# The head of a linear-attention and two-feed-forward kernel in another emission order

## The chip, the cores and the metric

The kernel runs on 1 core of one Trainium2 chip. The metric is device time in microseconds (us) of one execution; three runs of the kernel before took 870.92, 872.31 and 872.92 us.

## The reference

Inputs are r, k, v of shape (4, 8, 768, 48) (batch B, heads H, steps S, head width D), w and u of shape (8, 48), and two pairs of weight matrices. All is float32.

```
state = 0                                    # (B, H, 48, 48)
for t in range(768):
    cur = (u * k_t) outer v_t
    y_t = r_t @ (state + cur)
    state = w * state + k_t outer v_t
x = y as (3072 tokens, 384 features)
h = x @ w_in   (384 x 2048);  g = max(h, 0) + alpha * min(h, 0);  x = g @ w_out  (2048 x 384)
h = x @ w_in2  (384 x 2048);  g = h * tanh(log(1 + exp(h)));      out = g @ w_out2
```

## The kernel before, in words

**Attention in units.** The 768 steps are cut into 6 chunks of 128. Units 0 to 3 are the first chunk of the four batches; each has its own load of r and k (turned, `rk`), and of v and k (`nat`). From unit 4 on a unit is half a chunk (64 steps) of two batches. A unit is: scores r·k on TensorE (`scores`), a mask and the u-term put over them (`preset`, `masked`), the product with v (`attend0`, `batch`), and the running state (`states_first`, `t_decay`, `t_update`). The decay is carried by tables of powers of w that `tables` computes on VectorE; `load_RKs` (four DMAs from SBUF to SBUF) copies them from the layout of pairs of heads into the layout of seats that units from 4 on use.

**The feed-forward layers in slots.** A layer has 6 blocks of 512 tokens times 16 slices of the hidden width: 96 slots. A slot is `mA_h` (9 matmuls into a PSUM bank `h`), `mA_g` (ScalarE, then VectorE, from `h` to `g`; after it the bank is free), `mA_hi` and `mA_lo` (g split in two rounded parts, ScalarE and VectorE) and `mA_out` (9 matmuls). Block 0 needs units 0 to 3, so slot 0 starts when all four are through. There are two `h` banks, and a unit from 4 on takes one of them too, from its `batch` until `x_parts` has read it out.

**Weights.** Each of the 16 weight slices of layer 1 comes in raw (768 KB, `more_raw`, `load_raw`), is scaled on ScalarE (`w_scale`, two instructions), joined on VectorE (`w_join`) and split in two parts (`w_hi`, `w_lo`). From slot 15 on, the weights of layer 2 come the same way, one slice per four slots: `load_raw 1 f`, `w_scale (1,f)`, `w_join (1,f)`, `w2_store f` back to DRAM.

**Order.** Every step is a closure with a place in slots: `at(place, work, ...)` (L823). A dictionary `PLACES` (L60 on) replaces places by name, and `run_plan` (L833) sorts by place and calls the steps. The order of calls is the order in which instructions stand in each engine's queue, and each queue is worked off in order: a step that waits holds back all that stands behind it on its engine. All loads and stores of this part stand in one queue, that of SyncE (SP). Semaphores are set by the framework. Between two steps on different engines the order of calls matters only where one needs the other's data or buffer.

**Steps that the prediction follows.** `keep_warm` (L592) is a pair of filler matmuls; 8 calls stand ahead of everything, and 10 single calls are in `PLACES` as `keep_warm 3` with 0 to 9 marks `#`. `mA_end 0` (L646) copies the three sums of block 0 out of PSUM (ScalarE, VectorE, ScalarE) and stores them with one DMA. `t_decay 8` runs on ScalarE (four instructions, by the entry `?decay 8`), `preset 9 0` and `preset 9 1` on ScalarE (four each), `prep_c2 9` on VectorE (one sum).

```
    def run_plan():
        for place, _, work, args in sorted(plan, key=lambda p: p[:2]):
            work(*args)
```

Of the kernel before, what the change touches and what calls it, by code (L numbers as in the profile page):

```python
# [54 lines left out]
def more_state(u):  # L55
# [5 lines left out]
    "tables": -133.8283, "dma_start": -128.3432, "load_unit 1": -128.1527, "load_unit 0": -125.2362,  # L61
    "load_unit 2": -124.1803, "load_unit 3": -121.8174, "pad_v 1": -119.5623, "m_first 0": -118.998,
    "c_first 0": -117.2355, "dma_start#": -115.5868, "more_raw 3": -115.5854, "memset": -115.5721,
    "load_k 1": -115.4582, "tensor_scalar": -115.426, "dma_start##": -115.3727, "pad_v 0": -115.2759,
    "load_k 2": -115.0763, "load_k 0": -114.1881, "prep_rk 0": -113.5294, "keep_warm 3####": -111.4759,
    "<lambda> 0": -111.3741, "scale_Kn": -109.6007, "<lambda> 2": -108.8137, "w_scale (0,0)": -108.7521,
# [8 lines left out]
    "preset_first 2": -97.6565, "w_join (0,0)": -97.4588, "c_first 3": -97.3694, "w_hi (0,0) False": -96.6418,  # L75
# [7 lines left out]
    "half_tables": -88.7279, "preset 4 0": -86.4962, "x_first_lo 1": -85.1599, "w_hi (0,1) False": -84.3399,  # L83
# [3 lines left out]
    "mA_h 1": -10.0052, "w_hi (0,2) False": -9.0297, "scores 4": -7.6474, "w_join (0,3)": -7.6021,  # L87
# [4 lines left out]
    "w_lo (0,3)": 1.8993, "batch 4": 1.9228, "tables_seat": 1.9613, "mA_out 0": 2.0723, "w_join (0,4)": 2.1732,  # L92
    "mA_hi 1": 2.2917, "w_scale (0,5)": 2.2957, "mA_lo 1": 2.3517, "prep_kn 5": 2.3844, "prep_pair 6 0": 2.5634,
    "w_hi (0,4) False": 2.6901, "mA_h 2": 2.7398, "w_lo (0,4)": 2.8443, "mA_g 2": 2.9067, "w_join (0,5)": 2.9707,
    "more_raw 8": 2.9931, "more_raw 9": 3.0346, "t_decay 4": 3.0928, "mA_hi 2": 3.1982, "w_hi (0,5) True": 3.2114,
# [6 lines left out]
    "batch 5": 4.9611, "w_hi (0,6) False": 5.1766, "w_scale (0,8)": 5.2656, "more_raw 11": 5.4186, "mA_hi 5": 5.4234,  # L102
# [5 lines left out]
    "w_hi (0,9) True": 7.2287, "more_raw 13": 7.3665, "w_lo (0,8)": 7.3825, "mA_h 7": 7.4985, "mA_g 7": 7.5512,  # L108
    "masked 6 0": 7.5749, "w_lo (0,9)": 7.6299, "prep_c2 7": 7.6723, "mA_out 6": 7.7202, "mA_hi 7": 7.7615,
    "mA_lo 7": 7.9068, "w_join (0,10)": 7.9852, "preset 7 0": 7.9988, "mA_h 8": 8.1558, "prep_kn 6": 8.2758,  # L110
    "mA_g 8": 8.2832, "more_raw 14": 8.5104, "w_hi (0,10) False": 8.5586, "batch 6": 8.605, "x_parts 6": 8.6069,
# [6 lines left out]
    "w_hi (0,12) False": 11.0336, "prep_kn 7": 11.1115, "mA_hi 11": 11.1167, "w_lo (0,12)": 11.263,  # L118
# [3 lines left out]
    "batch 7": 12.4901, "w_hi (0,13) True": 12.5785, "x_parts 7": 12.6986, "load_unit 9": 12.7519,  # L122
# [935 lines left out]
```

## Time and profile before

| what | us |
|---|---|
| median of 3 runs | 872.31 (870.92 to 872.92) |
| profiled execution, its span from first to last instruction | 870.2 |
| TensorE (PE) busy in the span | 861.3 (99%) |
| VectorE (DVE) busy | 631.9 (73%) |
| ScalarE (ACT) busy | 616.2 (71%) |
| GpSimd (POOL) busy | 106.9 (12%) |

The profile shows one execution, of which it gives the span; what lies around the span is in the times of the runs. Busy PE includes the filler matmuls and the time in which a matmul is in flight. The chain of waits that ended last is 93% PE; its other parts (4% DMA) lie in the first 45 us. Each row of a timeline is: start us, length us, engine, source line, operation, out<-in, shapes, count, and in brackets the idle time of the engine before it and what ended it. Instructions of one engine overlap a little, so the distance from start to start is shorter than the length. "SPq" is SyncE's queue that issues DMAs.

### The profile page before, as it was taken

How to read it: one execution, taken by the hardware profiler on the slowest of the kernel's cores; microseconds unless marked ns; L12 is line 12 of the kernel's file. 1: busy time of each engine (PE TensorE's matmuls, PEld its weight loads, DVE VectorE, ACT ScalarE, POOL GpSimd, SP SyncE). 2: the span in 40 equal slices, each digit the busy share in tenths (PEclk: the TensorE clock that was granted, in tenths of full speed). 3: DMA queues.
4: the chain of work that ended last, by engine and by line, in shares of the span. 5: the costliest groups of instructions: out<-in, count | busy, mean ns of one | idle time of the engine just before them, and what ended most of it. 6: DMA issues, size and time to landing. Idle time of an engine off the chain costs nothing.

```text
span 870.2 us, 16712 instructions
## 1 busy us (share of the span) xinstructions
PE 861.3 (99%) x6380; PEld 712.1 (82%) x6380; DVE 631.9 (73%) x1012; ACT 616.2 (71%) x1174; POOL 106.9 (12%) x121
## 2 busy tenths in 40 slices
PE   9899999999999999999999999999999999999998
PEld 6678878888888888888888888888888888888897
DVE  6888855657656565554665887887887887887875
ACT  3797755454445545444555998998998998998886
POOL 4744222111122111100002000000000000000000
PEclk9999999999999999999999999999999999999999
DMA  8967464254444526211621200110110110100101
GB/s 317 277 210 216 111 195 140 82 170 157 136 131 141 143 86 209 77 56 64 205 87 35 110 1 1 26 48 1 26 48 1 24 51 0 27 12 1 26 12 37
DMA packets 65840, 80.41 MB, mean 92 GB/s; under 512 B 39712, under 2 KB 52960, under 8 KB 65760
## 3 DMA queue, kind: packets, MB, share of 16 engines
q1 hardware_dynamic: 65200, 79.24, 29.9%
q8 instruction: 50, 0.82, 0.4%
q14 instruction: 30, 0.25, 0.1%
q10 hardware_dynamic: 560, 0.10, 0.1%
HBM read 61.16 MB, written 15.73 MB: 88 GB/s over the span
## 4 chain that ended last, share of the span: by engine, by line
PE 93%; DMA 4%; ACT 1%; SPq 1%; DVE 0%; issue 0%; POOL 0%; ACTq 0%; DVEq 0%; POOLq 0%
PE h L238 44%; PE acc L643 22%; PE sc L764 8%; PE acc L764 8%; PE yt L764 4%; PE acc L762 3%; DMA rk<-in_rkT 1%; DMA nat<-in_nat 1%; PE sc L457 1%; PE sc L762 1%; DMA wrawr<-in_w 1%; PE h L488 1%; PE yt L509 1%; DMA w15u<-in_nat 1%; PE sc L502 1%; PE yt L488 1%
## 5 line engine op out<-in xcount | busy, mean ns | idle before, releaser
L238 PE MATMUL h<-x,w 128*128 128x512 f32 x1728 | 415.6, 390 | 2.3 <-DVE w L163 1.3
L238 PEld LDWEIGHTS h<-x,w 128*128 128x128 f32 x1728 | 323.8, 188 | 71.4 <-DVE w L163 2.1
L643 PE MATMUL acc<-ghi,w 128*128 128x512 f32 x516 | 175.2, 394 | 0.0
L611 ACT ACTIVATE m<-h 128x512 f32<-128x512 f32 x96 | 57.2, 596 | 87.5 <-PE h L238 87.4
L643 PEld LDWEIGHTS acc<-ghi,w 128*128 128x128 f32 x516 | 96.8, 188 | 21.3
L613 DVE SCALAR_TENSOR_TENSOR g<-m,oma,h 128x512 f32<-128x512 f32 x96 | 71.6, 746 | 57.7 <-ACT m L611 56.6
L160 ACT ACTIVATE ghi<-g 128x512 fp32r<-128x512 f32 x86 | 54.1, 629 | 76.1 <-PE acc L643 46.1
L643 PE MATMUL acc<-glo,w 128*128 128x512 f32 x258 | 100.5, 389 | 0.0
L163 DVE TENSOR_TENSOR glo<-g,ghi 128x512 fp32r<-128x512 f32 x86 | 60.2, 700 | 51.8 <-ACT ghi L160 51.7
L701 DVE SCALAR_TENSOR_TENSOR a<-ghi,h 128x512 f32<-128x512 f32 x96 | 66.1, 688 | 37.8 <-ACT ghi L698 31.3
L701 DVE SCALAR_TENSOR_TENSOR g<-s,c 128x512 f32<-128x512 f32 x95 | 66.7, 702 | 22.7 <-ACT s L698 20.6
L709 ACT ACTIVATE m<-h 128x512 f32<-128x512 f32 x96 | 56.4, 588 | 35.0 <-PE h L238 35.0
L163 DVE TENSOR_TENSOR gloB<-g,ghiB 128x512 fp32r<-128x512 f32 x105 | 72.0, 686 | 6.8 <-ACT ghiB L160 6.8
L698 ACT ACTIVATE ghi<-m,biases 128x512 f32<-128x512 f32 x96 | 69.6, 725 | 3.2
L160 ACT ACTIVATE ghiB<-g 128x512 fp32r<-128x512 f32 x105 | 64.8, 617 | 8.8 <-PE acc L643 6.9
L698 ACT ACTIVATE glo<-ghi,biases 128x512 f32<-128x512 f32 x96 | 68.1, 710 | 0.1
L698 ACT ACTIVATE s<-glo,biases 128x512 f32<-128x512 f32 x96 | 68.1, 709 | 0.0
L698 ACT ACTIVATE s<-s,biases 128x512 f32<-128x512 f32 x96 | 68.0, 708 | 0.0
L764 PE MATMUL sc<-ghiB,w 128*128 128x512 f32 x192 | 66.9, 389 | 0.0
L701 DVE SCALAR_TENSOR_TENSOR b<-ghi,a 128x512 f32<-128x512 f32 x96 | 65.7, 685 | 0.1
L701 DVE SCALAR_TENSOR_TENSOR c<-glo,b 128x512 f32<-128x512 f32 x95 | 65.7, 692 | 0.0
L764 PE MATMUL acc<-ghiB,w 128*128 128x512 f32 x192 | 61.7, 389 | 0.0
(184 smaller groups left out, 1161.3 us busy)
## 6 DMA issues: line engine op xcount, KB each, us to landing
wrawr<-in_w SPq DMA_DIRECT2D x28, 768.0 KB, 4.9
nat<-in_nat SPq DMA_DIRECT2D x40, 288.0 KB, 4.2
w2d<-wj SPq DMA_DIRECT2D x16, 384.0 KB, 2.5
wraw<-w2d SPq DMA_DIRECT2D x16, 384.0 KB, 3.0
rk<-in_rkT SPq DMA_DIRECT2D x40, 128.0 KB, 2.9
x2d<-xo SPq DMA_DIRECT2D x6, 768.0 KB, 3.4
x<-x2d SPq DMA_DIRECT2D x6, 768.0 KB, 4.4
rk<-in_rkT SPq DMA_DIRECT2D x40, 96.0 KB, 2.7
```

Of the source, the lines that this page charges most:

```text
L160: act.activation(out=hi, in_=src, func=AF.Copy)
L163: eng.tensor_tensor(out=lo, in0=src, in1=hi.bitcast(F32), op=ALU.subtract)
L238: pe.matmul(h, w_in(layer, f, a, c), x[:, b, c, :], start=(k == 0), stop=(k == 3 * KC - 1))
L488: pe.matmul(y[i][64 * q:64 * q + 64, p * HC:(p + 1) * HC], T[ROWS[h], 2 * bp + i, k, :], pair[i][ROWS[h], 0, k, t], start=(r == 0 and not ...
L611: act.activation(out=m, in_=hA[s], func=AF.Relu, scale=-1.0)
L613: dve.scalar_tensor_tensor(out=g, in0=m, scalar=oma[:, f:f + 1], in1=hA.pop(s), op0=ALU.mult, op1=ALU.add)
L643: pe.matmul(acc[0][c], w_out(0, f, a)[:, c * 128:(c + 1) * 128], g[b], start=(f == 0 and k == 0), stop=(f == NF - 1 and k == 2))
L698: act.activation(out=out, in_=in_, func=AF.Square, scale=scale, bias=fin[bias])
L701: dve.scalar_tensor_tensor(out=out, in0=in0, scalar=scalar, in1=in1, op0=op0, op1=ALU.mult)
L709: act.activation(out=bnew("t", n), in_=v["h", n], func=AF.Tanh, scale=0.5)
L762: pe.matmul(acc[1][t][:, :DM], g[a][:, t * C:(t + 1) * C], w_out(1, f, b), **se)
L764: pe.matmul(acc[1][t], w_out(1, f, a)[:, t * 128:(t + 1) * 128], g[b], **se)
```

## The change

Only `PLACES` changes: all entries for steps up to slot 18 get new places, between 1.699 and 17.999, 0.05 apart. The set of steps is the same, and so is everything from `mA_h 18` on. The order of the new dictionary is the order of the calls. Its core (lines left out are of the same kind):

```diff
-    "tables": -133.8283, "dma_start": -128.3432, "load_unit 1": -128.1527, "load_unit 0": -125.2362,
...
-    "m_first 3": -99.4133, "load_RKs": -98.9853, "scores 1": -98.8978, "preset_first 1": -98.86, "masked 1 0": -98.78,
...
-    "masked 8 0": 14.6804, "t_update 7": 14.7869, "mA_lo 14": 14.7896, "load_raw 1 0": 14.8571, "masked 8 1": 14.8651,
...
-    "mA_hi 16": 16.883, "prep_kn 9": 17.1837, "t_decay 8": 17.205, "preset 9 0": 17.3813, "preset 9 1": 17.3858,
-    "x_parts 8": 17.9208, "load_unit 11": 18.7912,
+    "?lo 2": 1, "?decay 4": 1, "?preset 3": 1, "?lo 4": 1, "load_unit 0": 1.699, "pad_v 0": 1.749, "tables": 1.799,
+    "scale_Kn": 1.849, "m_first 0": 1.899, "c_first 0": 1.949, "load_unit 1": 1.999, "<lambda> 1": 2.049,
...
+    "masked 2 1": 4.399, "masked 2 0": 4.449, "load_k 2": 4.499, "c_first 3": 4.549, "load_RKs": 4.599,
+    "keep_warm 3##": 4.649, "keep_warm 3########": 4.699, "keep_warm 3#": 4.749, "scores 3": 4.799, "w_lo (0,0)": 4.849,
...
+    "load_unit 4": 5.899, "prep_pair 4 0": 5.949, "dma_start#": 5.999, "tensor_scalar": 6.049, "prep_kn 1": 6.099,
+    "states_first 0": 6.149, "half_tables": 6.199, "keep_warm 3###": 6.249, "keep_warm 3#########": 6.299,
+    "keep_warm 3": 6.349, "load_unit 5": 6.399, "x_first_lo 3": 6.449, "w_hi (0,2) False": 6.499, "more_raw 7": 6.549,
+    "x_first_lo 1": 6.599, "mA_h 0": 6.649, "mA_h 1": 6.699, "tables_seat": 6.749, "prep_pair 4 1": 6.799,
...
+    "w_join (0,4)": 7.699, "more_raw 8": 7.749, "more_raw 9": 7.799, "more_raw 10": 7.849, "keep_warm 3#####": 7.899,
+    "keep_warm 3#######": 7.949, "mA_hi 1": 7.999, "prep_c 5": 8.049, "mA_lo 1": 8.099, "mA_g 2": 8.149,
...
+    "prep_kn 8": 16.899, "mA_hi 15": 16.949, "mA_lo 15": 16.999, "mA_g 16": 17.049, "masked 8 1": 17.099,
+    "mA_out 15": 17.149, "mA_end 0": 17.199, "load_raw 1 0": 17.249, "mA_hi 16": 17.299, "mA_lo 16": 17.349,
+    "batch 8": 17.399, "x_parts 8": 17.449, "w_scale (1,0)": 17.499, "w_join (1,0)": 17.549, "prep_c2 9": 17.599,
+    "preset 9 0": 17.649, "preset 9 1": 17.699, "prep_kn 9": 17.749, "t_decay 8": 17.799, "t_update 8": 17.849,
+    "mA_g 17": 17.899, "mA_hi 17": 17.949, "w2_store 0": 17.999, "load_unit 11": 18.7912,
```

Steps that had no entry before keep their place by rule there: `mA_h 17` 17, `mA_g 17` 17.55, `mA_out 15` 17.68, `mA_end 0` 17.681, `w_scale (1,0)` and `w_join (1,0)` 17.69. With that, the queues near slot 18 read:

```
PE  before:  ... mA_out 14, batch 8, mA_h 17, mA_out 15, mA_h 18, mA_out 16, mA_h 19
PE  after:   ... mA_out 14, mA_h 17, mA_out 15, batch 8, mA_h 18, mA_out 16, mA_h 19
ACT before:  t_decay 8, preset 9 0, preset 9 1, mA_g 17, mA_end 0, w_scale (1,0), mA_hi 17, x_parts 8, mA_g 18
ACT after:   mA_end 0, mA_hi 16, x_parts 8, w_scale (1,0), preset 9 0, preset 9 1, t_decay 8, mA_g 17, mA_hi 17, mA_g 18
DVE after:   mA_end 0, mA_lo 16, x_parts 8, w_join (1,0), prep_c2 9, t_update 8, mA_g 17, mA_lo 17
SP  before:  load_unit 9, load_unit 10, load_raw 1 0, mA_end 0, w2_store 0, x_parts 8, load_unit 11
SP  after:   load_unit 9, load_unit 10, mA_end 0, load_raw 1 0, x_parts 8, w2_store 0, load_unit 11
```

And near slot 0, from `attend0 3` on:

```
PE  before:  attend0 3, states_first 0, keep_warm, mA_h 0, mA_h 1, scores 4, states_first 2, batch 4, mA_out 0, mA_h 2, mA_out 1
PE  after:   attend0 3, states_first 0, 3 keep_warm, mA_h 0, mA_h 1, scores 4, mA_h 2, 2 keep_warm, mA_out 0, batch 4, mA_out 1
```

In the queue before, all 10 `keep_warm` calls stand ahead of `mA_h 0`; in the queue after, 8 of them. `states_first 2` stands ahead of `mA_h 0` after.

## Rows read from the trace of the kernel before

**Rows 1.** Busy time by stretch: length, busy us (count) by engine, granted clock, DMA.

```profile
9.06:32.59 23.53, 23.36 (x334) 17.68 (x332) 18.66 (x23) 12.48 (x34) 13.56 (x13) 1.00 0.97 309
43.67:119.33 75.66, 74.86 (x808) 61.12 (x802) 61.46 (x101) 58.25 (x129) 29.74 (x26) 1.00 0.59 176
```

**Rows 2.** Timeline of PE ahead of slot 0: a filler call, scores, states.

```profile
19.72 0.89 PE L596 MATMUL acc<-ghi 128*128 128x384 f32 x2
20.55 1.10 PE L457 MATMUL sc<-w12u 48*64 48x64 f32 x32
...
31.31 0.53 PE L538 MATMUL acc<-w9u 128*48 128x48 f32 x16
...
32.13 0.91 PE L596 MATMUL acc<-ghi 128*128 128x384 f32 x2
```

**Rows 3.** Timeline of PE from slot 0 to slot 4: where it waited.

```profile
36.83 1.89 PE L238 MATMUL h<-x,w 128*128 128x512 f32 x7 [1.27 <-DVE w L163]
39.66 0.69 PE L457 MATMUL sc<-rk 48*64 48x64 f32 x32 [0.94 <-DVE rk L381]
40.29 0.56 PE L538 MATMUL acc<-w13u 128*48 128x48 f32 x16
...
41.63 0.27 PE L488 MATMUL h<-rk,T 48*64 48x64 f32 x1 [0.42 <-DVE g L613]
...
43.67 0.50 PE L643 MATMUL acc<-ghi,w 128*128 128x512 f32 x1
...
52.94 0.93 PE L238 MATMUL h<-x,w 128*128 128x512 f32 x3 [0.80 <-DVE x L163]
```

**Rows 4.** Timeline of DVE: the first product with the seats' tables.

```profile
34.11 1.80 DVE L381 TENSOR_TENSOR rk<-rk,RKs 112x1024 f32<-112x1024 f32 x1 [1.50 <-DMA RKs<-RK]
```

**Rows 5.** Timeline of PE around batch 8 and slots 15 to 18.

```profile
113.03 0.27 PE L488 MATMUL h<-rk,T 48*64 48x64 f32 x1
...
114.94 2.35 PE L238 MATMUL h<-x,w 128*128 128x512 f32 x9
117.13 0.39 PE L643 MATMUL acc<-ghi,w 128*128 128x512 f32 x1
...
119.17 2.20 PE L238 MATMUL h<-x,w 128*128 128x512 f32 x9
```

**Rows 6.** Timeline of SyncE's queue at the end of block 0.

```profile
109.88 0.58 SPq L180 DMA_DIRECT2D wrawr<-in_w  x1
119.99 0.34 SPq L653 DMA_DIRECT2D x2d<-xo  x1
122.53 0.32 SPq L214 DMA_DIRECT2D w2d<-wj  x1
```

**Rows 7.** Raw loads issued at 89.90 and at 109.88: us to landing.

```profile
DMA to landing us min/median/max: 4.3/4.3/4.3
DMA to landing us min/median/max: 6.3/6.3/6.3
```

**Rows 8.** Timeline of ACT around the end of block 0.

```profile
114.51 1.17 ACT L518 ACTIVATE T<-T,w 112x96 f32<-112x96 f32 x4 [0.48 <-PE h L488]
115.59 2.02 ACT L428 ACTIVATE Ah<-cst,cc 128x64 f32<-128x64 f32 x8
...
119.86 0.89 ACT L186 ACTIVATE wrawr<-wrawr 128x768 f32<-128x768 f32 x1
120.65 0.87 ACT L187 ACTIVATE wrawr<-wrawr 128x768 uint32<-128x768 uint32 x1
...
121.93 0.21 ACT L160 ACTIVATE y<-yt 112x64 fp32r<-112x64 f32 x1
...
122.56 0.62 ACT L611 ACTIVATE m<-h 128x512 f32<-128x512 f32 x1
```

**Rows 9.** Timeline of DVE: a sum for the u-term, then the end of block 0.

```profile
30.36 0.55 DVE L416 TENSOR_REDUCE cc<-nat 128x8 f32<-128x384 f32 x1
...
121.55 0.96 DVE L192 SCALAR_TENSOR_TENSOR wj<-wrawr 128x768 uint32<-128x768 uint32 x1 [2.07 <-ACT wrawr L187]
...
123.14 0.35 DVE L163 TENSOR_TENSOR x<-h,x 112x192 fp32r<-112x192 f32 x1
...
125.14 0.74 DVE L613 SCALAR_TENSOR_TENSOR g<-m,oma,h 128x512 f32<-128x512 f32 x1
```

**Rows 10.** Busy time after the last matmul: PE busy 0.00, granted clock 0.92.

```profile
868.00:870.30 2.30, 0.00 (x0) 0.00 (x0) 0.00 (x0) 0.00 (x0) 0.00 (x0) 0.92 0.32 106
```

More of the change, by code (lines that the diff above doesn't have):

```diff
@@ L60 @@
 PLACES = {
-    "tables": -133.8283, "dma_start": -128.3432, "load_unit 1": -128.1527, "load_unit 0": -125.2362,
[L62 to L65, printed above, removed]
@@ L66 @@
-    "<lambda> 0": -111.3741, "scale_Kn": -109.6007, "<lambda> 2": -108.8137, "w_scale (0,0)": -108.7521,
[8 rows of a table removed]
-    "preset_first 2": -97.6565, "w_join (0,0)": -97.4588, "c_first 3": -97.3694, "w_hi (0,0) False": -96.6418,
[7 rows of a table removed]
-    "half_tables": -88.7279, "preset 4 0": -86.4962, "x_first_lo 1": -85.1599, "w_hi (0,1) False": -84.3399,
[3 rows of a table removed]
-    "mA_h 1": -10.0052, "w_hi (0,2) False": -9.0297, "scores 4": -7.6474, "w_join (0,3)": -7.6021,
[4 rows of a table removed]
-    "w_lo (0,3)": 1.8993, "batch 4": 1.9228, "tables_seat": 1.9613, "mA_out 0": 2.0723, "w_join (0,4)": 2.1732,
@@ L93 @@
-    "mA_hi 1": 2.2917, "w_scale (0,5)": 2.2957, "mA_lo 1": 2.3517, "prep_kn 5": 2.3844, "prep_pair 6 0": 2.5634,
-    "w_hi (0,4) False": 2.6901, "mA_h 2": 2.7398, "w_lo (0,4)": 2.8443, "mA_g 2": 2.9067, "w_join (0,5)": 2.9707,
-    "more_raw 8": 2.9931, "more_raw 9": 3.0346, "t_decay 4": 3.0928, "mA_hi 2": 3.1982, "w_hi (0,5) True": 3.2114,
[6 rows of a table removed]
-    "batch 5": 4.9611, "w_hi (0,6) False": 5.1766, "w_scale (0,8)": 5.2656, "more_raw 11": 5.4186, "mA_hi 5": 5.4234,
[5 rows of a table removed]
-    "w_hi (0,9) True": 7.2287, "more_raw 13": 7.3665, "w_lo (0,8)": 7.3825, "mA_h 7": 7.4985, "mA_g 7": 7.5512,
@@ L109 @@
-    "masked 6 0": 7.5749, "w_lo (0,9)": 7.6299, "prep_c2 7": 7.6723, "mA_out 6": 7.7202, "mA_hi 7": 7.7615,
-    "mA_lo 7": 7.9068, "w_join (0,10)": 7.9852, "preset 7 0": 7.9988, "mA_h 8": 8.1558, "prep_kn 6": 8.2758,
-    "mA_g 8": 8.2832, "more_raw 14": 8.5104, "w_hi (0,10) False": 8.5586, "batch 6": 8.605, "x_parts 6": 8.6069,
[6 rows of a table removed]
-    "w_hi (0,12) False": 11.0336, "prep_kn 7": 11.1115, "mA_hi 11": 11.1167, "w_lo (0,12)": 11.263,
[3 rows of a table removed]
-    "batch 7": 12.4901, "w_hi (0,13) True": 12.5785, "x_parts 7": 12.6986, "load_unit 9": 12.7519,
@@ L123 @@
-    "mA_hi 12": 12.8252, "w_hi (0,14) False": 12.9398, "mA_out 11": 12.9799, "w_lo (0,14)": 12.9935,
-    "w_lo (0,13)": 13.2622, "w_scale (0,15)": 13.3173, "prep_c 9": 13.3735, "mA_h 13": 13.5197, "mA_h 14": 13.5472,
-    "w_join (0,15)": 13.6724, "w_hi (0,15) True": 13.8183, "load_unit 10": 13.8272, "mA_lo 12": 13.8955,
[7 rows of a table removed]
+    "?pair 8 0": 1, "?hi 7": 1, "?hi 3": 1, "?decay 8": 1, "?hi 15": 1, "?decay 9": 1, "?warm 5": 1, "?lo 13": 1,
+    "?lo 2": 1, "?decay 4": 1, "?preset 3": 1, "?lo 4": 1, "load_unit 0": 1.699, "pad_v 0": 1.749, "tables": 1.799,
@@ new lines @@
+    "scale_Kn": 1.849, "m_first 0": 1.899, "c_first 0": 1.949, "load_unit 1": 1.999, "<lambda> 1": 2.049,
+    "preset_first 0": 2.099, "load_k 0": 2.149, "m_first 1": 2.199, "c_first 1": 2.249, "preset_first 1": 2.299,
+    "prep_rk 1": 2.349, "dma_start": 2.399, "table_Kn 0": 2.449, "prep_rk 0": 2.499, "scores 0": 2.549,
+    "load_unit 2": 2.599, "m_first 2": 2.649, "c_first 2": 2.699, "masked 0 0": 2.749, "masked 0 1": 2.799,
+    "load_unit 3": 2.849, "m_first 3": 2.899, "keep_warm 3####": 2.949, "more_raw 3": 2.999, "w_scale (0,0)": 3.049,
@@ new lines @@
+    "keep_warm 3######": 3.099, "pad_v 2": 3.149, "dma_start##": 3.199, "pad_v 3": 3.249, "prep_rk 2": 3.299,
[3 rows of a table added]
+    "x_first 0": 4.149, "w_scale (0,1)": 4.199, "w_join (0,1)": 4.249, "w_hi (0,0) False": 4.299, "scores 2": 4.349,
[6 rows of a table added]
+    "load_unit 4": 5.899, "prep_pair 4 0": 5.949, "dma_start#": 5.999, "tensor_scalar": 6.049, "prep_kn 1": 6.099,
+    "states_first 0": 6.149, "half_tables": 6.199, "keep_warm 3###": 6.249, "keep_warm 3#########": 6.299,
+    "keep_warm 3": 6.349, "load_unit 5": 6.399, "x_first_lo 3": 6.449, "w_hi (0,2) False": 6.499, "more_raw 7": 6.549,
[6 rows of a table added]
@@ new lines @@
+    "mA_out 0": 8.199, "w_hi (0,3) True": 8.249, "w_lo (0,3)": 8.299, "w_scale (0,5)": 8.349, "w_join (0,5)": 8.399,
+    "load_unit 7": 8.449, "w_hi (0,4) False": 8.499, "prep_kn 4": 8.549, "batch 4": 8.599, "x_parts 4": 8.649,
[4 rows of a table added]
+    "mA_h 4": 9.699, "mA_g 4": 9.749, "mA_out 2": 9.799, "mA_out 3": 9.849, "w_hi (0,5) True": 9.899,
[3 rows of a table added]
+    "w_join (0,8)": 10.699, "w_hi (0,7) True": 10.749, "w_lo (0,7)": 10.799, "mA_hi 5": 10.849, "mA_lo 5": 10.899,
+    "prep_kn 5": 10.949, "batch 5": 10.999, "mA_g 6": 11.049, "t_decay 5": 11.099, "t_update 5": 11.149,
@@ new lines @@
+    "w_scale (0,9)": 11.199, "x_parts 5": 11.249, "mA_hi 6": 11.299, "mA_lo 6": 11.349, "w_hi (0,8) False": 11.399,
[4 rows of a table added]
+    "w_hi (0,9) True": 12.449, "w_hi (0,10) False": 12.499, "w_lo (0,10)": 12.549, "preset 6 1": 12.599,
+    "masked 6 1": 12.649, "prep_c2 7": 12.699, "mA_g 8": 12.749, "mA_hi 8": 12.799, "prep_kn 6": 12.849,
+    "mA_lo 8": 12.899, "batch 6": 12.949, "w_lo (0,9)": 12.999, "t_decay 6": 13.049, "w_scale (0,12)": 13.099,
+    "w_join (0,12)": 13.149, "w_scale (0,11)": 13.199, "w_join (0,11)": 13.249, "w_hi (0,11) True": 13.299,
[3 rows of a table added]
@@ L133 @@
+    "mA_out 10": 14.149, "w_hi (0,12) False": 14.199, "w_lo (0,12)": 14.249, "mA_h 12": 14.299, "w_join (0,13)": 14.349,
[4 rows of a table added]
+    "mA_out 12": 15.399, "prep_c 8": 15.449, "w_hi (0,14) False": 15.499, "w_lo (0,14)": 15.549, "mA_h 14": 15.599,
+    "mA_g 13": 15.649, "w_scale (0,15)": 15.699, "w_join (0,15)": 15.749, "mA_hi 13": 15.799, "mA_lo 13": 15.849,
+    "mA_out 13": 15.899, "w_hi (0,15) True": 15.949, "w_lo (0,15)": 15.999, "mA_h 15": 16.049, "mA_h 16": 16.099,
[8 rows of a table added]
 }
```

76 rows, old and new, of the table PLACES are left out of this document.

## The prediction

> **What bounds the kernel now.** The page comes first: PE is busy 861.3 of 870.2 us, the next engine 631.9, and the chain of waits is PE for 93%. Nothing that only shortens work on another engine can show. Then the busy time by stretch: from 9.06 to 32.59 us PE is busy 23.36 of 23.53, fillers included, and from 43.67 to 119.33, 74.86 of 75.66 [rows 1]. In such a stretch the end of the kernel is the sum of PE's work, so an order can change the time in two ways only: it takes away a place where PE waits, or it makes one. The third view, PE's timeline, tells where it waits before: between the two stretches, 1.27 us ahead of the second half of `mA_h 1`, 0.94 ahead of `scores 4`, 0.42 ahead of `batch 4`, and 0.80 at 52.94 [rows 3]. These are 3.4 us in all, and the change moves steps around each of them. The last views are the queues at slots 15 to 19, where PE does not wait before; there I look for waits that the new order makes.
>
> **The head: what goes.** Up to `mA_h 0` PE has the same work in both orders but for two things: `states_first 2` comes ahead of it (+0.82, from 31.31 to 32.13) and two filler calls go behind it (2 × 0.83, from 19.72 to 20.55) [rows 2]. If PE waits nowhere, `mA_h 0` starts at 32.59 + 0.82 − 1.66 = 31.75.
>
> The first three waits have one origin. DVE's first product with the seats' tables stood 1.50 us for the copies RK to RKs [rows 4]; behind it in DVE's queue stood `w_lo (0,1)`, for which `mA_h 1` waited, and out of it come `scores 4` and `batch 4`. After, `load_RKs` is issued ahead of unit 4's loads instead of behind them, and `w_lo (0,1)` stands ahead of the product. So I cost the three waits at nothing. From `mA_h 0` on PE then has three `h` (a set of 9 matmuls goes 2.04 from start to start, 117.13 to 119.17 [rows 5]), `scores 4` (0.63, 39.66 to 40.29 [rows 3]) and two fillers (1.66): 6.12 + 0.63 + 1.66 = 8.41, and `mA_out 0` starts at 40.16 against 43.67 [rows 3]. By then the one order has done `mA_h 2` and the other `states_first 2` and `batch 4`, of about equal length (2.04 between 41.63 and 43.67), so the two can be compared: 3.5 ahead. The wait of 0.80 at 52.94, for unit 4's `x_parts`, goes too, as `batch 4` and `x_parts 4` now stand ahead of the step that needs their bank: 4.3, the upper bound.
>
> Against this: with two fillers fewer ahead of `mA_h 0`, and unit 0's r and k first, a wait that a filler covered can come out anywhere between 9 and 32 us (a filler hides 0.83), and in slots 3 to 9 four weight slices stand close behind the step before them. The lower bound I take is 0.5, where only the 0.80 goes and 0.3 of it comes back. I take 3.0, near the upper end, because DVE's row names the origin and the new order removes just that.
>
> **The end of block 0: what comes.** Call T the modelled end of `mA_out 15`, 119.33 before [rows 1]; `batch 8` (1.91, 113.03 to 114.94 [rows 5]) now stands behind it, so T comes earlier after, and I count from it.
>
> *SyncE's queue.* Before, layer 2's first raw weights were asked for at 109.88, and the store of block 0's sums at 119.99, 0.66 behind T, as it needs those sums [rows 6]. After, the raw load stands behind that store, in one queue that works in order. It is issued at T + 0.66 + 0.34 = T + 1.0. Raw loads took 4.3 us and 6.3 us to land [rows 7]; the store is in flight beside this one, so I take 5.7: T + 6.7, where before it had landed 3.2 us ahead of T.
>
> *ScalarE and VectorE.* Behind that load stand, in order, `w_scale (1,0)` (1.66, 119.86 to 121.52 [rows 8]) to T + 8.4; `w_join` (0.96 [rows 9]) to T + 9.4; behind it on DVE `prep_c2 9` (0.55 [rows 9]) to T + 9.95; the presets that read its sum (2.02 [rows 8]) to T + 12.0; `t_decay 8` (1.17 [rows 8]) to T + 13.1; and only then `mA_g 17`, 0.62 on ACT and 0.74 on DVE [rows 8, 9]: T + 14.4. Until this end the bank of `mA_h 17` is not free, and `mA_h 19` needs it. Before, `mA_g 17` stood ahead of `mA_end 0` and `w_scale` on ACT.
>
> *PE.* `batch 8` runs to T + 1.8. `mA_h 18` needs its bank back, through `x_parts 8`: 1.56 from ACT's start to DVE's end (121.93 to 123.49 [rows 8, 9]), so T + 3.3, a wait of 1.5. `mA_h 18` and `mA_out 16` (4.08) run to T + 7.4. `mA_h 19` waits from there to T + 14.4: 7.0. What is late next is `mA_out 17`, but `mA_hi` and `mA_lo 17` have `mA_h 19`'s 2.04 us to run in. Sum: 1.5 + 7.0 = +8.5. From slot 20 on the order is the old one, and PE, being the bound, can give none of it back.
>
> **The clock.** The granted clock is 1.00 in both stretches of PE's work [rows 1], short waits among them. It is 0.92 over the last 2.3 us, in which no matmul ran [rows 10], so an idle PE does fall from 2.4 to the lower level, 1.2 GHz. A wait of 7.0 is three times that row's length, so I expect a fall ahead of `mA_h 19`. No row shows how long PE then stays slow. Nothing, if the clock is back at once; 4.1, if `mA_h 19` and `mA_out 17` (4.08) both run at half rate. I take 2.0.
> [...]
>
> **Sum.** −3.0 + 8.5 + 2.0 = +7.5. The profiled execution has a span of 870.2, the median is 872.31: 2.1 us lie around the span, and nothing in the change touches them. So 872.3 + 7.5 = 879.8. Own range: with a gain of 4.3, a load of 4.3 us (1.4 earlier) and no clock term, 872.3 − 4.3 + 7.1 = 875.1; with a gain of 0.5, a load of 6.3 and 4.1 for the clock, 872.3 − 0.5 + 9.1 + 4.1 = 885.0.
>
> **Rivals.**
> *A: the raw load is not held by the store* (SyncE issues it early all the same). Then `w_scale (1,0)` starts once `x_parts 8` has left ACT, at about T + 2.6, and everything behind it shifts by 4.1: `mA_g 17` ends at T + 10.3, PE waits 1.5 + 2.9 = 4.4, and the clock keeps 1.00 as it did over 1.27. 872.3 − 3.0 + 4.4 = 873.7. For it: nothing but that a framework may split queues. Against it: the rows of the store and of the loads carry the same queue's name [rows 6]. It decides if `w_scale (1,0)` starts by T + 2.7; each us later costs one.
> *B: the head gives nothing.* A wait that the two fillers covered comes back in full, or `RKs` is late for another reason. 872.3 + 8.5 + 2.0 − 0 = 882.8. For it: the DMA engines are busy 0.97 of the head [rows 1], so that a load put first makes another one late. Against it: the loads of the head are the same, and PE's rows there stand close.
> *C: `mA_h 18` gets the bank of `mA_h 17`, not that of `batch 8`.* Then all of the chain up to T + 14.4 stands ahead of `mA_h 18`: from T + 1.8 PE waits 12.6, with the same clock term. 872.3 − 3.0 + 12.6 + 2.0 = 883.9. It follows from the order in which banks are handed out; taking them in turn gives my forecast.
> *D: faster.* Mechanism: layer 2's chain does not stand ahead of `mA_g 17` in effect, since ACT has `mA_g 17` done before `w_scale (1,0)` is called for. Then `mA_h 19` does not wait, and what is left is the gain of the head and the wait of 1.5 for `x_parts 8`: 872.3 − 3.0 + 1.5 = 870.8; with the head's upper bound, 869.5. Its place is ACT's queue at slot 17, its price 8.5, and it decides if `mA_g 17` ends by T + 7.4. For it: `w_scale (1,0)` makes weights that no step reads before slot 96. Against it: ACT's queue after, in which it is the fourth of the steps there and `mA_g 17` the eighth.
>
> **How the numbers follow.** 0.2% of the time is 1.74 us, about what a measurement of this kernel can tell from no change; within it is 870.6 to 874.0. The forecast has 0.58, A 0.10, B 0.11, C 0.08, D 0.13. The forecast, B and C are all slower: 0.77; A lies at the edge, 0.04 slower and 0.06 within; D is 0.08 faster and 0.05 within. Slower 0.81, within 0.11, faster 0.08. The range goes from 872.5, which takes in most of A, to 885.0, the forecast's upper bound, which holds B and C; what it leaves out is D and little more.
>
> **What would show it.** Right: `mA_out 0` starting near 40.2, `mA_h 1` without a wait for `w_lo (0,1)`; in SyncE's queue the store x2d and, about 0.4 us later, the raw load; ACT waiting some 4 us on a DMA ahead of `w_scale (1,0)`; PE waiting 1.5 ahead of `mA_h 18` and 7 ahead of `mA_h 19`, released by DVE's L613; a granted clock below 1.00 in the stretch behind. Wrong: a raw load issued ahead of the store (A), PE's first long wait ahead of `mA_h 18` (C), no wait over 2 us at slot 19 (D), or `mA_out 0` at 43 or later (B).

## The result, and the profile after

The changed kernel takes 881.88 us (median of 4 runs, 879.14 to 884.25) against 872.07 for the kernel before (4 runs): a ratio of 1.0116, interval 1.0092 to 1.014. The forecast was 879.8, range 872.5 to 885.0. The profiled execution has a span of 880.8, 10.6 over that of before.

The first view is PE's waits, as sums (engine, line, waited for: us, times, longest):

```profile
PE h L233 <- DVE g L608: 4.6, 1, 4.6
PE h L233 <- DVE x L158: 1.8, 1, 1.8
PE acc L591 <- POOL ghi L883: 1.3, 1, 1.3
PE yt L483 <- POOL T L487: 0.3, 1, 0.3
```

The waits of [rows 3] are gone, as forecast, and two new ones stand in first place; the last two stand before as well. The sum of the new ones, 6.4, is not the 10.6. What is missing shows only in lengths. This is PE's timeline in the head and in slots 15 to 20; `h` x9 is 2.2 us long where nothing is wrong [rows 5]:

```profile
8.97 0.95 PE L394 MATMUL yt<-ut,glo 112*128 112x2 f32 x8
...
11.19 1.10 PE L452 MATMUL sc<-w8u 48*64 48x128 f32 x32
12.42 1.36 PE L394 MATMUL h<-ut,ghi 112*128 112x2 f32 x8
13.64 3.33 PE L591 MATMUL acc<-ghi 128*128 128x384 f32 x4
16.91 1.99 PE L452 MATMUL sc<-w10u 48*64 48x64 f32 x32
...
36.89 4.57 PE L233 MATMUL h<-x,w 128*128 128x512 f32 x18
...
46.14 0.47 PE L638 MATMUL acc<-ghi,w 128*128 128x512 f32 x1
...
117.96 0.39 PE L638 MATMUL acc<-ghi,w 128*128 128x512 f32 x1
...
122.02 3.88 PE L233 MATMUL h<-x,w 128*128 128x512 f32 x9 [1.76 <-DVE x L158]
...
132.58 3.85 PE L233 MATMUL h<-x,w 128*128 128x512 f32 x9 [4.60 <-DVE g L608]
...
138.33 2.20 PE L233 MATMUL h<-x,w 128*128 128x512 f32 x9
```

Two filler calls (x4) at 13.64 take 3.33 us; before, two calls at 9.88 took 1.86. The next scores take 1.99 instead of 1.10 [rows 2]. No idle time stands at any of them. The view by stretch says why (columns as in [rows 1]); the last two stretches are the wait ahead of `mA_h 19` and the slot behind it:

```profile
8.97:13.64 4.67, 4.54 (x61) 4.15 (x60) 4.64 (x6) 0.92 (x4) 3.42 (x4) 0.93 1.04 422
...
14.00:23.50 9.50, 9.44 (x84) 6.87 (x85) 6.42 (x6) 3.13 (x9) 2.25 (x4) 0.51 0.94 316
...
127.98:132.58 4.60, 0.00 (x1) 0.01 (x1) 1.40 (x4) 3.58 (x14) 0.00 (x0) 0.99 0.92 251
132.58:138.33 5.75, 5.75 (x19) 4.62 (x19) 4.36 (x6) 2.32 (x4) 0.00 (x0) 0.71 0.27 107
```

PE is busy 9.44 of 9.50 us from 14.00 to 23.50, and the granted clock is 0.51: nearly all of it at 1.2 GHz. Before, the same stretch has 1.00. Ahead of it, from 8.97 to 13.64, PE ran one narrow product after another (2 to 128 columns) with no filler among them. Before, four filler calls stand among the same products:

```profile
9.88 1.86 PE L596 MATMUL acc<-ghi 128*128 128x384 f32 x4
...
12.70 0.91 PE L596 MATMUL acc<-ghi 128*128 128x384 f32 x2
...
14.26 0.89 PE L596 MATMUL acc<-ghi 128*128 128x384 f32 x2
```

The price of the low clock is 9.5 × (1 − 0.51) = 4.7 us.

The end of block 0 in the queues of SyncE, then ScalarE, then VectorE answers to [rows 6, 8, 9]:

```profile
119.00 0.34 SPq L648 DMA_DIRECT2D x2d<-xo  x1
119.38 0.43 SPq L175 DMA_DIRECT2D wrawr<-in_w  x1
...
124.94 0.92 ACT L181 ACTIVATE wrawr<-wrawr 128x768 f32<-128x768 f32 x1 [3.85 <-DMA wrawr<-in_w]
125.75 0.90 ACT L182 ACTIVATE wrawr<-wrawr 128x768 uint32<-128x768 uint32 x1
128.14 2.02 ACT L423 ACTIVATE Ah<-cst,cc 128x64 f32<-128x64 f32 x8 [1.49 <-DVE cc L411]
130.06 1.15 ACT L513 ACTIVATE T<-T,w 112x96 f32<-112x96 f32 x4
131.12 0.57 ACT L606 ACTIVATE m<-h 128x512 f32<-128x512 f32 x1
...
126.68 0.96 DVE L187 SCALAR_TENSOR_TENSOR wj<-wrawr 128x768 uint32<-128x768 uint32 x1 [4.81 <-ACT wrawr L182]
127.56 0.55 DVE L411 TENSOR_REDUCE cc<-nat 128x8 f32<-128x384 f32 x1
...
131.78 0.74 DVE L608 SCALAR_TENSOR_TENSOR g<-m,oma,h 128x512 f32<-128x512 f32 x1
```

The raw load stands 0.38 behind the store, ScalarE waits 3.85 for it, and the rest follows in the order of the queue. `mA_g 17` ends at 132.52 and PE's `mA_h 19` starts at 132.58.

### The profile page after: what moved, and what is told of

It is laid out like the page before. It is cut to its first block, busy times and chain, and to the rows that moved or that the text cites. A ratio compares the mean times of both kernels' runs of the same rounds, so it can differ in the third digit from the quotient of the medians.

```text
span 880.8 us, 16716 instructions
## 1 busy us (share of the span) xinstructions
PE 868.6 (99%) x6380; PEld 717.8 (81%) x6380; DVE 631.8 (72%) x1012; ACT 617.4 (70%) x1174; POOL 101.7 (12%) x121
## 4 chain that ended last, share of the span: by engine, by line
PE 98%; ACT 1%; DMA 1%; issue 0%; DVE 0%; POOL 0%; SPq 0%; POOLq 0%; ACTq 0%
PE h L233 45%; PE acc L638 23%; PE sc L759 7%; PE acc L759 7%; PE yt L759 4%; PE acc L757 3%; PE acc L591 2%; PE sc L452 2%; PE sc L757 1%; PE h L483 1%; PE yt L504 1%; PE sc L497 1%; DMA wrawr<-in_w 1%; PE yt L483 1%; PE h L467 0%; PE yt L467 0%
```

## The experiments

All times are medians beside the kernel before on the same chip (870.4 to 871.0 there); each edit is a handful of places laid over the dictionary.

**e1: fillers between the narrow products of the head.**

```diff
-}
+} | {"keep_warm 3####": 1.96, "keep_warm 3######": 2.27, "keep_warm 3##": 2.56, "keep_warm 3########": 2.71}
```

> After, with four of the ten filler calls moved from behind the narrow products of the head to between them (TensorE's work is the same, only in another order). Theory 1: the head lost its time because the granted clock stood at 1.2 GHz from about 14 to 23.5 us, after 4.7 us of narrow products without a filler; with fillers between them the clock stays at 1.00, mA_h 0 starts at about 32.0 to 32.5 instead of 36.89, mA_out 0 at 40.5 to 41.5 instead of 46.14, and the time falls by about 4.5 to 5: 877. Theory 2: the head is late because unit 0's loads, or VectorE's tables, come late; then TensorE shows waits where the slow products stood, mA_h 0 stays at 36 or later, and the time is within 1 us of 881.9.

879.01, ratio 1.0093 (1.008 to 1.0106). The stretch from 14.00 to 23.50, and PE's timeline in the head and in slots 18 to 20:

```profile
14.00:23.50 9.50, 9.50 (x162) 7.84 (x150) 8.12 (x9) 5.92 (x13) 5.32 (x7) 1.00 0.96 318
```

```profile
25.14 1.10 PE L452 MATMUL sc<-w14u 48*64 48x64 f32 x32 [1.18 <-DVE A L456]
...
32.95 4.59 PE L233 MATMUL h<-x,w 128*128 128x512 f32 x18
...
42.22 0.47 PE L638 MATMUL acc<-ghi,w 128*128 128x512 f32 x1
...
118.09 2.29 PE L233 MATMUL h<-x,w 128*128 128x512 f32 x9 [1.76 <-DVE x L158]
128.64 4.21 PE L233 MATMUL h<-x,w 128*128 128x512 f32 x9 [6.22 <-DVE g L608]
135.22 2.21 PE L233 MATMUL h<-x,w 128*128 128x512 f32 x9
```

Theory 1 holds: clock 1.00, and `mA_h 0` and `mA_out 0` are 3.9 us earlier. That is still 0.5 and 0.7 later than the latest places expected, as a wait of 1.18 for VectorE comes out ahead of `scores 3`, where the slow products had left none. The time falls by less, since `mA_h 19` and `mA_out 17` now take 6.58 (128.64 to 135.22) instead of 5.75: 3.9 − 0.8 = 3.1, which is the difference of the two spans (880.8 − 877.7). By the ratios the two kernels differ by 0.2%, and the intervals overlap, so this reading rests on the traces and not on the times.

**e5: the same fillers taken away from the kernel before.**

```diff
-}
+} | {"keep_warm 3####": -97.7, "keep_warm 3######": -97.69, "keep_warm 3##": -97.68, "keep_warm 3########": -97.67}
```

> Before, with four filler calls that stood between the first narrow products moved together behind scores 1 and the first product with v; TensorE's work is the same. Theory 1 (the fillers hold the clock): the granted clock falls to 1.2 GHz at about 13 to 14 us and stays there for up to 10 us, mA_h 0 starts 3 to 5 us later than 32.59 and the time rises by 3 to 5: 876. Theory 2 (fillers only fill waits): the clock stays at 1.00 and the time is within 1 us of 872.1.

874.46, ratio 1.004 (1.0028 to 1.0052). Where the clock falls, the stretch in which it is low, and PE's timeline:

```profile
11.00:11.50 0.50, 0.50 (x5) 0.45 (x5) 0.50 (x1) 0.00 (x0) 0.23 (x1) 0.99 1.08 424
11.50:12.00 0.50, 0.04 (x1) 0.00 (x0) 0.50 (x2) 0.37 (x2) 0.00 (x0) 0.50 1.11 467
...
14.00:24.50 10.50, 10.33 (x74) 7.04 (x75) 4.89 (x6) 3.57 (x10) 4.78 (x5) 0.63 0.87 280
```

```profile
13.29 1.87 PE L399 MATMUL h<-ut,ghi 112*128 112x2 f32 x8 [1.75 <-DVE ghi L391]
...
38.48 4.59 PE L238 MATMUL h<-x,w 128*128 128x512 f32 x18
```

The clock falls here too, in an order that has nothing else of the change. It falls at 11.5, where the narrow products end and a wait of 1.75 for VectorE begins, so the wait did not bring it about. Not all of the loss is clock, which costs 10.5 × (1 − 0.63) = 3.9 here: the 1.75 is a wait that the fillers had covered. `mA_h 0` is 5.9 later than before's 32.59, the time only 3.4: `mA_h 1` and `scores 4` now wait for nothing, so the 1.27 and 0.94 of [rows 3] come off, 5.9 − 2.2 = 3.7. These two waits, then, also go when PE merely comes late.

**e2: the two issues in SyncE's queue swapped back in the kernel after.**

```diff
-}
+} | {"load_raw 1 0": 16.76}
```

> After, with one pair of issues in SyncE's queue swapped: the raw load of layer 2 ahead of the store of block 0's sums. Theory 1 (the load held behind the store makes the chain late): w_scale (1,0) starts behind x_parts 8 at about 121.0 instead of 124.94, the wait of 4.60 ahead of mA_h 19 falls to about 0.7, the wait of 1.76 ahead of mA_h 18 stays, and if a short wait leaves the clock alone mA_h 19 takes 2.2 instead of 3.85: 881.9 - 3.9 - 1.6 = 876.4. Theory 2 (ScalarE's order alone, whatever the load does): w_scale still starts where it did and the time stays within 1 us of 881.9.

878.93 (875.31 to 881.14), ratio 1.0088 (1.007 to 1.0106), so the time alone barely tells it from the kernel after. The timelines of ScalarE and PE do:

```profile
122.37 0.92 ACT L181 ACTIVATE wrawr<-wrawr 128x768 f32<-128x768 f32 x1
...
123.44 2.31 PE L233 MATMUL h<-x,w 128*128 128x512 f32 x9 [1.76 <-DVE x L158]
130.03 2.99 PE L233 MATMUL h<-x,w 128*128 128x512 f32 x9 [2.25 <-DVE g L608]
...
135.86 2.20 PE L233 MATMUL h<-x,w 128*128 128x512 f32 x9
```

`w_scale` stands right behind `x_parts 8` without a wait. With T at 119.76 it starts at T + 2.6 and `mA_h 19` at T + 10.3, as rival A had them; in the kernel after `mA_h 19` starts at T + 14.2. So the load behind the store costs 3.9 us of the chain, and ScalarE's order the rest. I expected a shorter wait and a full clock behind it, 876.4; the clock fell after 2.25 too (`mA_h 19` 2.99 instead of 2.2, and with `mA_out 17` 5.83 instead of 4.08), and this execution stood 1.51 in the head at an instruction where the profile shows no releaser.

**e4: the same swap made in the kernel before.**

```diff
-}
+} | {"load_raw 1 0": 17.685}
```

> Before, with one pair of issues in SyncE's queue swapped: the raw load of layer 2 behind the store of block 0's sums. Theory 1 (a load held behind the store costs by what stands behind w_scale on ScalarE): issued at 120.4, landed near 126, w_scale to 127.7, then mA_hi 17 and x_parts 8, which give back the bank of batch 8: mA_h 19 starts at about 130 instead of 123.63 and runs at half rate; 871.0 + 6.4 + 1.7 = 879. Theory 2 (the raw load has slack, since layer 2's weights are not read before slot 96): within 1 us of 871.0.

878.61, ratio 1.0088 (1.0075 to 1.0102):

```profile
125.99 0.88 ACT L186 ACTIVATE wrawr<-wrawr 128x768 f32<-128x768 f32 x1 [5.90 <-DMA wrawr<-in_w]
...
129.74 4.18 PE L238 MATMUL h<-x,w 128*128 128x512 f32 x9 [6.21 <-DVE x L163]
```

One swap of two issues costs 7.8 us: PE waits 6.2, and `mA_h 19` and `mA_out 17` take 6.5 (129.74 to 136.23) instead of 4.08; these add up to 8.6 in the profiled execution, whose time, 880.39, is 1.8 above the median. So the load has no slack here, however late its data is wanted: what stands behind `w_scale` in ScalarE's queue pays.

**e3: the steps that free the bank of `mA_h 17` moved ahead, the load left where it is.**

```diff
-}
+} | {"mA_hi 16": 17.11, "mA_lo 16": 17.12, "mA_g 17": 17.13, "mA_hi 17": 17.46, "mA_lo 17": 17.47}
```

> After, with mA_hi 16, mA_lo 16 and mA_g 17 moved ahead of mA_out 15, and mA_hi 17 and mA_lo 17 ahead of w_scale (1,0); the load stays behind the store. Theory 1 (the two waits at slots 18 and 19 come from h banks held by steps that stand behind others on ScalarE): mA_h 18 takes the bank of mA_h 17 and starts right behind batch 8, mA_h 19 takes that of batch 8; neither waits over 0.3, both take 2.2 at full clock, and the time falls by 1.8 + 4.6 + 1.7 + 1.65 = 9.7: 872.2. ScalarE still waits about 4 us on the raw load. Theory 2 (the late weights hold TensorE by another way, such as the presets of unit 9 for batch 9): a wait of 2 us or more turns up behind slot 19, and the time stays above 875.

878.66, ratio 1.0093 (1.0078 to 1.0107). Theory 1 failed:

```profile
118.04 2.35 PE L233 MATMUL h<-x,w 128*128 128x512 f32 x9
...
122.27 2.20 PE L233 MATMUL h<-x,w 128*128 128x512 f32 x9
...
131.62 4.21 PE L233 MATMUL h<-x,w 128*128 128x512 f32 x9 [5.11 <-DVE g L608]
```

`mA_h 18` and `mA_h 19` no longer wait, and `mA_h 20` waits 5.11, released by the same line: now `mA_g 18` stands behind the late `w_scale`. The wait had moved one slot.

**e8: the whole end of block 0 mended, the head as after.**

```diff
-}
+} | {"mA_hi 16": 17.11, "mA_lo 16": 17.12, "mA_g 17": 17.13, "mA_hi 17": 17.46, "mA_lo 17": 17.47,
+     "load_raw 1 0": 16.76, "prep_c2 9": 17.451, "t_decay 8": 17.471, "preset 9 0": 17.472, "preset 9 1": 17.473}
```

> After, with the end of block 0 mended and the head as it is: raw load ahead of the store, mA_hi 16, mA_lo 16, mA_g 17 ahead of mA_out 15, mA_hi 17 and mA_lo 17, then t_decay 8 and the presets of unit 9 ahead of w_scale (1,0). Theory 1 (the waits of slots 18 to 20 are the whole loss at this end): no wait over 0.5 there, the clock at 1.00 from 30 us on, and 881.1 - 9.7 = 871.4, which is before's 871.0 plus the 1.1 us by which the slow head comes in late, less what slots 1 to 4 give. Theory 2: the wait moves one more slot behind, and the time stays above 874.

873.5, ratio 1.0035 (1.0025 to 1.0045): by the ratios 0.8% back, some 7 us of the 9.7 expected; the time lies between the two theories. Two waits are left in the timeline, and the clock stays at 1.00 behind them:

```profile
130.06 2.37 PE L233 MATMUL h<-x,w 128*128 128x512 f32 x9 [0.82 <-DVE g L608]
133.63 0.27 PE L483 MATMUL h<-rk,T 48*64 48x64 f32 x1 [1.21 <-DVE g L608]
```

The other part of the rest is the head, and it differs between executions: the two runs with a mean granted clock of 0.998 and 1.00 took 872.08 and 872.15, the five at 0.993 and 0.994 took 874.92 to 875.79. The profiled execution, one of the five, has 0.58 over 14.00 to 23.50 and 1.00 from 30 us on; the first two have no trace, but fit a head that kept its clock.

**e9: e1, and the two filler calls ahead of `mA_out 0` moved ahead of `scores 3`.**

```diff
-}
+} | {"keep_warm 3####": 1.96, "keep_warm 3######": 2.27, "keep_warm 3##": 2.56, "keep_warm 3########": 2.71,
+     "keep_warm 3#####": 4.56, "keep_warm 3#######": 4.57}
```

> After with the fillers of e1, and the two filler calls that stood ahead of mA_out 0 moved ahead of scores 3, where e1 waited 1.2 us for VectorE. Theory 1 (those two hold up mA_out 0, whose operands were there at 40.1 in e1): mA_out 0 starts 1.3 to 1.8 earlier than e1's 42.22, at about 40.6, near the 40.2 that was forecast, and the time is 879.0 - 1.5 = 877.5, as the loss at slots 18 and 19 is still there. Theory 2 (mA_out 0 waits for its operands anyway): 879.0.

877.02, ratio 1.0069 (1.0058 to 1.0081), 2.0 under e1. `mA_out 0` starts earlier than was forecast for the change:

```profile
39.70 0.39 PE L638 MATMUL acc<-ghi,w 128*128 128x512 f32 x1
```

So a filler costs its length at the one place, ahead of `mA_out 0`, and nothing at the other, where it covers a wait: e1's 1.18 ahead of `scores 3` is gone.

**e7: e9's fillers and e8's end together.**

```diff
-}
+} | {...the entries of e9..., ...the entries of e8...}
```

> After with both mendings (e9's fillers and e8's end of block 0). If the two losses are separate and the rest of the new order gains what was forecast: mA_out 0 at about 40.6, no wait over 0.5 at slots 18 to 20, clock 1.00 all through, and 877.5 - 10 = 867.5, faster than before by 3.5 (before's 871.0 less 3.0 to 3.9). If the new order has another loss that these two covered: 870 or more.

869.54, ratio 0.9984 (0.9975 to 0.9992): faster than before, but by 1.3 and not 3.5, between the two stated outcomes. The waits behind slot 18, among PE's waits as sums:

```profile
...
PE h L483 <- DVE g L608: 1.2, 1, 1.2
PE h L233 <- DVE g L608: 0.8, 1, 0.8
...
```

**e10: e7 with `w_scale (1,0)`, `w_join (1,0)` and `w2_store 0` behind `mA_hi 18`.**

```diff
+     "w_scale (1,0)": 18.81, "w_join (1,0)": 18.82, "w2_store 0": 18.83}
```

> The kernel of e7 with w_scale (1,0), w_join (1,0) and w2_store 0 behind mA_hi 18. Theory 1 (what is left of the loss in e7, waits of 0.84 ahead of mA_h 20 and 1.22 behind it, both released by VectorE's mA_g, is the 1.6 us of w_scale and 0.96 of w_join standing ahead of mA_g 18): both waits go and the time is 869.5 - 2.0 = 867.5, 0.4% under before. Theory 2 (mA_g 18 is late by the products with the tables and t_update on VectorE, which stay ahead of it): the waits stay within 0.5 of what they were, and the time stays at 869.5.

868.06, ratio 0.9973 (0.9962 to 0.9984): 2.3 us faster than before, and by the two ratios 1.4% under the kernel after. The wait of 0.8 is gone, of 1.2 there remain 0.7, so Theory 1 holds in the main:

```profile
...
PE h L483 <- DVE g L608: 0.7, 1, 0.7
...
```

## Why the prediction was right, and where it was wrong

*The end of block 0* was right step by step. With T at 118.35 (117.96 + 0.39): the load issued at T + 1.0 (forecast 1.0), `w_scale` starts at T + 6.6 (6.7), `w_join` done at T + 9.3 (9.4), the presets done at T + 11.8 (12.0), `t_decay 8` at T + 12.9 (13.1), `mA_g 17` at T + 14.2 (14.4). e2 and e4 show that the swapped issues are the cause, e3 and e8 that the order on ScalarE passes it on. The sum of the waits, 6.4 instead of 8.5, is not a fault of the chain: `mA_h 18` ran at half rate (3.88), which the forecast did not have, and that time came off the next wait. In e1, where it ran at full rate, the same wait is 6.22.

*The clock's term* was 2.0, chosen between 0 and 4.1. `mA_h 19` and `mA_out 17` took 5.75 instead of 4.08: 1.7. The choice between the bounds had no row behind it, so that it came out near is luck. In e1, e4 and e9, with waits of 6.2 to 6.3, it is 2.5, 2.4 and 2.2.

*The head* was wrong, by sign: −3.0 was forecast, and T came 0.9 us later than before (118.35 against 119.33 − 1.91 = 117.42). `mA_out 0` was even 2.5 late (46.14 against 43.67); the slots up to T gave 1.5 of it back, 0.8 by the wait at 52.94. The step that failed is "If PE waits nowhere, `mA_h 0` starts at 31.75". PE stood idle for 0.4 us in all between 8.97 and 36.89, and `mA_h 0` started at 36.89: a filler call was priced at the 0.83 that it lasts, and the forecast looked at the clock only where PE stands idle. The fillers among the narrow products held the clock, and without them it stood at 1.2 GHz for most of 9.5 us (4.7 us). e1 gives 3.9 of the 5.1 back, e5 takes the clock from the kernel before in the same way. The two fillers ahead of `mA_out 0` were priced too low as well, at 1.66 where they took 1.95 us (44.19 to 46.14). The 2.04 that the prediction gives to `states_first 2` and `batch 4` is `batch 4` alone; both orders have done `states_first 2` by then, so its sum stands. The rest of the head's reasoning stands: the waits of [rows 3] went, and since `mA_h 0` starts at 32.4 in e9 and 32.1 in e7, near before's 32.59, it is the order that takes them away there and not lateness as in e5. With the fillers placed so, `mA_out 0` starts at 39.7 and 39.4, 4 us ahead of before.

*Why the total came out near all the same*, though the head failed: T came 3.9 later than forecast, the chain is 0.2 shorter and the clock 0.3 cheaper, and `mA_h 19` before was itself 0.4 behind the sum (123.63, where 119.17 + 4.08 = 123.25): 7.5 + 3.9 − 0.2 − 0.3 − 0.4 = 10.5, against the 10.6 by which the spans differ. By the medians it is 9.8. That the total lies in the range, with a term wrong by 3.9, is in part luck: the range was wide enough for a head that gives nothing, and the loss of the head differs between executions. The four runs of the kernel after took 879.14 at a mean granted clock of 0.996, 881.25 at 0.992, and 882.5 and 884.25 at 0.990; the first fits a head that kept its clock, as all of e1's runs have 0.996 too, but it has no trace.

*The rivals.* By the prediction's own sign (`mA_out 0` at 43 or later) the outcome is B's, and its 882.8 is nearer to 881.88 than the forecast's 879.8, but not by B's mechanism: B named the fillers as the danger, yet as cover for waits, and no wait came out in the kernel after. A's numbers (T + 2.6, T + 10.3) were measured in e2, so its condition was the right one and not met. C and D did not happen: PE's long wait stands ahead of `mA_h 19`, not `mA_h 18`, and it is there.

## What to carry to other kernels

When a step moves, price what it did to its neighbours and not its own length: a DMA issue by all that stands behind its reader on the reader's engine, a filler matmul by the clock that it held. In a stretch where an engine is busy throughout, read the lengths of like instructions and the granted clock as well as the waits, for a loss of 4.7 us stood there with 0.06 us of idle time. A wait that is mended by moving one reader can turn up a slot later at the next (e3), so look at the whole queue behind the late step.

## What the runs showed of the hardware

- The granted clock fell while PE was hardly idle: 0.93 over 8.97 to 13.64, of which PE was busy 4.54 of 4.67 us with narrow products alone, and 0.51 over 14.00 to 23.50. With fillers among the same products it stayed at 1.00 (e1). How long it stayed low differed between executions with the same head: 0.51, 0.56, 0.58 and 0.80 over 14.00 to 23.50 in the kernel after, e2, e8 and e3. The times of the kernel after and of e8 go with it; e7 and e10, at 0.999 to 1.00 in all their runs, spread over about 2 us only.
- The same wait of 1.76 ahead of `mA_h 18` was followed by 3.88 us at the lower clock in the kernel after and by 2.3 at the full one in e1, e2 and e9. Waits of 0.8 and 1.2 (e7, e8) cost no clock, one of 2.25 (e2) did. What tells the fall behind 1.76 from the three cases without one stays open.
